# The opening of a Fourier-mixing and hard-swish kernel: zero fills on ScalarE, a third piece buffer, single small transfers, and weight conversions a piece behind, five of them inside chunk 0

## The chip, the cores and the metric

One core of a Trainium2 chip. The metric is the device time of one execution in microseconds (us), lower is better. Traces come from one profiled execution of each kernel, and times in them are us from the first instruction.

## The reference, cut to what matters

```python
x = (8, 3008, 256) float32; w_in = (256, 2048); w_out = (2048, 256)
X = np.fft.fft(np.fft.fft(x, axis=1), axis=2).real      # mixing
h = X.reshape(24064, 256) @ w_in
out = (h * np.clip(h + 3, 0, 6) / 6) @ w_out            # (24064, 256)
```

The Fourier transform along the sequence is done in two stages (47 x 64 = 3008). The transform along the 256 channels is folded into `w_in`; `w_out` is turned into seven blocks `G`. Weights are read as 64-bit floats, so each piece is converted on the chip before use.

## The kernel before

The batch is worked in four pairs, each pair in twelve chunks, each chunk in eight steps. A step of the steady part: TensorE makes `u` and `v` (8 matmuls), VectorE and ScalarE make the gated `a`, GpSimd adds parts of `a` into `c`, and TensorE accumulates 14 matmuls. This repeats from about 119 us to the end. Ahead of it stands the opening, where the change is:

```python
for b in range(2):                                   # zero halves of the tables T
    nc.vector.memset(T[(1 - b) * N2:(2 - b) * N2, b], 0.0)
...
for c in range(NXC):                                 # stage 1, eight pieces
    if c + 2 < NXC:
        load_x(first, c + 2)                         # rows and, by a gather, their partners
    load_w(c + 2)
    exponent_a(c)                                    # ScalarE: PM
    fold...                                          # VectorE
    if c > 0:
        join(c - 1)                                  # VectorE: mantissa x exponent
    mantissa(c)                                      # VectorE, two instructions
    for i in range(XC // 2):
        stage1...(first, c, i)                       # TensorE, then evict_z on ScalarE
    exponent_b(c)                                    # TensorE: scores ex
    exponent_c(c)                                    # ScalarE on ex
    if c in (2, 4, 6):
        use_pair(c // 2 - 1)                         # fold_w_in (TensorE) or mix_w_out (VectorE)
load_g(first, 0); load_g(first, 1); load_t(1)
for j in range(NXC, 14):                             # pieces 8 to 13, between the stages
    load_w(j + 2); exponent_a(j); exponent_b(j)
    if j > NXC:
        exponent_c(j - 1)
    join(j - 1); mantissa(j)
    if j % 2 == 0:
        use_pair(j // 2 - 1)
exponent_c(13); join(13); use_pair(6)
...                                                  # stage 2, then chunk 0 with pieces 14 and 15
```

A piece is converted in five moves: ScalarE writes exponent bits into `PM` (`exponent_a`), TensorE makes the scores `ex` of them (`exponent_b`), ScalarE makes a power of two of each (`exponent_c`), VectorE cuts out the mantissa `top` (`mantissa`, two instructions) and multiplies the two (`join`). A pair of pieces then goes through a "fold" of `w_in` (eight matmuls `wps`) or a "mix" of `w_out`. `mix_w_out` is four VectorE instructions, three subtractions and an addition, with both inputs in SBUF; for short I call them subtractions. `ex` takes one of the three score banks that `u` and `v` use. `evict_z` copies a stage-1 result to a buffer `z` (two of them), stores it, and writes one turned column through `zc` with two small transfers:

```python
def evict_z(pr, c, i, ps):
    if i == 0:
        pr.z[c] = zpool.tile([PZ, XC, D], F32, tag="z", name="z")
    ...
def turn_column(pr, c, z):
    zc = zpool.tile([PZ, XC], F32, tag="zc", name="zc")
    nc.scalar.activation(zc[:, 0:n], z[:, 0:n, P], AF.Identity, scale=...)
    for ci in range(2):
        nc.sync.dma_start(out=to[1 - ci, :, 0:n], in_=zc[ci::2, 0:n])
```

## Time and profile before

| | before |
|---|---|
| median of 3 runs | 2009.34 us (2008.16 to 2011.23) |
| span of the profiled run | 2005.7 us |
| first stage-1 matmul | 13.59 |
| last store of stage 1 issued | 58.10 |
| first matmul of stage 2 | 84.08 |
| first gate operation of VectorE ("S0") | 87.89 |
| eighth accumulation of chunk 0 begins ("A7") | 134.74 |

"Cold" below is TensorE at about half the granted clock (0.5 in the windows), "warm" at the full one. I split A7 into S0, the length of the opening, and A7 - S0 = 46.85, the length of chunk 0. The prediction shows the lines of the profile.

### The profile page before, as it was taken

Reading aid. Unit: us, or ns where it says so; the run is one execution under the profiler, and the core shown is the slowest. Engines: PE = TensorE matmul, PEld = TensorE weight load, DVE = VectorE, ACT = ScalarE, POOL = GpSimd, SP = SyncE. Lnnn points to the kernel's source line nnn. Section 1 sums busy time; section 2 is a strip of 40 time slices with the busy share of each in tenths; the row PEclk is TensorE's granted clock in tenths of the full one; section 3 lists DMA queues with packets and bytes.
Section 4 is the critical chain, followed back from the end, with each engine's and each line's share of the span. In section 5 each row is a group of like instructions: output and inputs, shape, how many; then the busy total and the mean of one; then the engine's idle time right before and its main releaser. Section 6 shows DMA issues by size and latency. Waiting matters only on the chain.

```text
span 2005.7 us, 28349 instructions
## 1 busy us (share of the span) xinstructions
PE 1962.5 (98%) x9144; PEld 1686.7 (84%) x9144; DVE 1444.6 (72%) x2707; ACT 694.7 (35%) x1196; POOL 1419.3 (71%) x1612
## 2 busy tenths in 40 slices
PE   8799999999999999999999999999999999999997
PEld 4388888888888888888888888888888888888886
DVE  6677767776777676777777777777678777777775
ACT  5433333333333333333333333333333333333322
POOL 3277778786677787777658877778666667667665
PEclk8899999999999999999999999999999999999999
DMA  9502211111111122210111221112110101101100
GB/s 294 143 21 56 59 39 47 49 47 35 27 35 50 40 49 53 54 51 25 41 26 29 67 55 42 51 43 52 35 27 19 27 17 26 33 12 27 27 12 19
DMA packets 159560, 93.52 MB, mean 47 GB/s; under 512 B 131595, under 2 KB 144395, under 8 KB 159414
## 3 DMA queue, kind: packets, MB, share of 16 engines
q1 hardware_dynamic: 149942, 58.23, 11.6%
q0 software_dynamic: 9472, 33.49, 6.0%
q8 instruction: 74, 1.21, 0.3%
q14 instruction: 72, 0.59, 0.1%
HBM read 54.32 MB, written 37.33 MB: 46 GB/s over the span
## 4 chain that ended last, share of the span: by engine, by line
PE 92%; DVE 3%; ACT 1%; issue 1%; POOL 0%; SPq 0%; DMA 0%; DVEq 0%; POOLq 0%; ACTq 0%
PE acc L378 55%; PE v L324 16%; PE u L324 16%; PE ps L279 2%; PE ps L226 2%; DVE a L356 1%; ACT t L353 1%; DVE u L337 1%; DVE s L329 1%; PE wps L520 0%; ACT PM L456 0%; DVE o L404 0%; DVE v L343 0%; PE awake L537 0%; PE ps L223 0%
## 5 line engine op out<-in xcount | busy, mean ns | idle before, releaser
L368 POOL TENSOR_TENSOR c<-a 128x512 f32<-128x512 f32 (+1 forms) x384 | 478.9, 1247 | 446.4 <-PE acc L378 361.3
L378 PE MATMUL acc<-c,G 128*128 128x256 f32 (+1 forms) x3072 | 712.1, 375 | 0.0
L353 ACT ACTIVATE t<-u,half 128x512 f32<-128x512 f32 (+2 forms) x416 | 272.3, 654 | 1101.1 <-DVE u L337 1089.5
L378 PEld LDWEIGHTS acc<-c,G 128*128 128x128 f32 x3072 | 577.5, 190 | 72.7
L329 DVE SCALAR_TENSOR_TENSOR s<-qn,WN,u 128x256 f32<-128x256 f32 x768 | 334.5, 477 | 351.6 <-PE u L324 348.8
L378 PE MATMUL acc<-a,G 128*128 128x256 f32 (+1 forms) x2304 | 550.6, 374 | 0.0
L378 PEld LDWEIGHTS acc<-a,G 128*128 128x128 f32 x2304 | 433.8, 190 | 57.4
L324 PE MATMUL v<-q,W 127*128 127x256 f32 x1536 | 397.0, 380 | 8.0 <-DVE a L356 8.0
L324 PE MATMUL u<-q,W 128*128 128x256 f32 x1536 | 394.3, 379 | 0.0
L324 PEld LDWEIGHTS v<-q,W 127*128 127x128 f32 x1536 | 289.5, 190 | 55.7 <-PE u L324 8.4
L324 PEld LDWEIGHTS u<-q,W 128*128 128x128 f32 x1536 | 287.3, 190 | 57.8 <-issue 13.9
L356 DVE SCALAR_TENSOR_TENSOR a<-t,u 128x512 f32<-128x512 f32 (+2 forms) x416 | 266.2, 646 | 95.2 <-ACT t L353 90.5
L368 POOL TENSOR_TENSOR c<-c,a 128x256 f32<-128x256 f32 (+1 forms) x384 | 275.2, 717 | 30.1
L368 POOL TENSOR_TENSOR c<-a,c 128x256 f32<-128x256 f32 (+1 forms) x384 | 275.0, 716 | 30.1
L337 DVE TENSOR_TENSOR u<-s,v 128x512 f32<-128x512 f32 (+1 forms) x384 | 263.0, 685 | 41.1 <-DVE s L329 1.4
L353 ACT ACTIVATE t<-v,half 128x512 f32<-128x512 f32 (+1 forms) x384 | 257.0, 669 | 5.8 <-DVE v L343 4.3
L343 DVE TENSOR_TENSOR v<-v,s 128x512 f32<-128x512 f32 (+1 forms) x384 | 257.7, 671 | 1.1
L356 DVE SCALAR_TENSOR_TENSOR a<-t,v 128x512 f32<-128x512 f32 (+1 forms) x416 | 255.2, 620 | 0.4 <-ACT t L353 0.2
L368 POOL TENSOR_TENSOR r<-w,e 128x256 f32<-128x256 f32 (+1 forms) x96 | 92.2, 981 | 3.8
L384 ACT ACTIVATE e<-acc 128x512 f32<-128x512 f32 (+1 forms) x192 | 86.9, 542 | 2.9 <-PE acc L378 2.8
L404 DVE STREAM_TRANSPOSE o<-r 128x256 f32<-128x256 f32 (+1 forms) x192 | 72.4, 414 | 6.4 <-POOL r L368 6.4
L236 ACT COPY z<-ps 96x512 f32<-96x512 f32 x64 | 36.9, 581 | 82.4 <-PE ps L226 64.1
(81 smaller groups left out, 750.2 us busy)
## 6 DMA issues: line engine op xcount, KB each, us to landing
out_dram<-o SPq DMA_DIRECT2D x736, 32.0 KB
zd<-z SPq DMA_DIRECT2D x32, 384.0 KB
g<-zd SPq DMA_DIRECT2D x48, 256.0 KB
xt<-in_x_dram POOLq DMA_DIRECT2D x21, 384.0 KB, 3.8
qn<-qd SPq DMA_DIRECT2D x23, 256.0 KB
st<-in_moe_w_in_dram POOLq DMA_DIRECT2D x8, 512.0 KB, 9.6
st<-in_moe_w_out_dram POOLq DMA_DIRECT2D x8, 512.0 KB, 5.2
xt<-in_x_dram POOLq DMA_DIRECT2D x7, 376.0 KB, 3.9
```

Source lines behind the costliest of these rows:

```text
L226: nc.tensor.matmul(ps[0:PZ], F[0:PR, 0:PZ], y[:, 2 * i:2 * i + 2, :], start=True, stop=True)
L279: nc.tensor.matmul(ps[:, blk, 2 * u:2 * u + 2], g[:, kk, blk * (P + 1):blk * (P + 1) + P], T[:, :, gr, blk, kk], start=True, stop=True)
L324: nc.tensor.matmul(ps[:, i], W1[r, blk, f * P:(f + 1) * P], q[r, blk, of:of + KC], start=True, stop=True)
L329: nc.vector.scalar_tensor_tensor(s[:, i].rearrange("p k n -> p (k n)"), qn[:, of * N2:(of + KC) * N2], WN[:, f:f + 1], u[:, i].rearrange(" ...
L337: nc.vector.tensor_tensor(u[:, :, 0:ns], s[:, :, 0:ns], v[:, :, 0:ns], op=AL.add)
L343: nc.vector.tensor_tensor(v[:, :, 0:nm], v[:, :, 0:nm], s[:, :, 0:nm], op=AL.subtract)
L353: nc.scalar.activation(t, h, AF.Relu, bias=half[:], scale=scale)
L356: nc.vector.scalar_tensor_tensor(dst, t, 1.0, h, op0=AL.min, op1=AL.mult)
L368: nc.gpsimd.tensor_tensor(out, in0, in1, op=AL.add)
L378: nc.tensor.matmul(ch.acc[i // 2][:, i % 2, 0:ch.n], G[:, i, fc, :], mv, start=(fc == 0 and i % 2 == 0), stop=(fc == NF - 1), skip_group_c ...
L384: nc.scalar.mul(ch.e[:, k:i + 1, 0:ch.n], ch.acc[i // 2][:, 0:i + 1 - k, 0:ch.n], 1.0 / WS)
L404: nc.vector.transpose(o[:, 0:n // DH, h], ch.r[:, m, h, 0:n].rearrange("p (j i) -> p j i", i=DH))
```

## The change

Its intent: start TensorE sooner and warm (fills to ScalarE, piece 0 issued first), not let stores hold ScalarE (third buffer, taken from the idle pool `g`), save issue time (one small transfer), and shorten the stretch between the stages by converting only pieces 7 to 10 there, and 11 to 15 inside chunk 0. The diff also lets `load_g` issue its two rows before its two columns. Core of the diff, with cuts:

```diff
+            pool, tag = (gpool, "g") if pr.p == 0 and c % 3 == 2 else (zpool, "z")
+            pr.z[c] = pool.tile([PZ, XC, D], F32, tag=tag, name="z")
...
-        for ci in range(2):
-            nc.sync.dma_start(out=to[1 - ci, :, 0:n], in_=zc[ci::2, 0:n])
+        nc.sync.dma_start(out=pr.zq[:, :, ::-1, cs].rearrange("b k c n -> (b k) c n"), in_=zc[:, 0:n])
...
-    nc.vector.memset(PM[:], 0x6400)
+    nc.vector.memset(PM[:]....bitcast(I32), 0x64006400)     # and ahead of the table cast
...
-        nc.vector.memset(T[(1 - b) * N2:(2 - b) * N2, b], 0.0)
+        nc.scalar.copy(t, Z[r].unsqueeze(1).to_broadcast([N2, NG, 2 * TB]))
...
+    BEHIND = [0, 1, 2, 3, 4, None, 5, 6]
+    # issue order: piece 0, w 0, piece 1, w 1, piece 2, w 2; load_t(0) after piece 0
+    def next_weights(j):
+        done = pending.pop() if pending else None
+        if done is not None:
+            exponent_c(done)
+        if j is not None:
+            exponent_a(j)
+            mantissa(j)
+        if done is not None:
+            join(done)
+        if j is not None:
+            exponent_b(j)
+            pending.append(j)
+        if done is not None and done % 2:
+            use_pair(done // 2)
...
+    for j in range(7, 11):
+        if j + 3 < 16:
+            load_w(j + 3)
+        next_weights(j)
...
+            for t, j in enumerate([11, 12, 13, 14, 15, None]):   # steps 0 to 5 of chunk 0
+                after.setdefault(t, []).append((next_weights, (j,)))
```

More of the change, by code (lines that the diff above doesn't have):

```diff
@@ L230, in evict_z @@
         if i == 0:
-            pr.z[c] = zpool.tile([PZ, XC, D], F32, tag="z", name="z")
+            pool, tag = (gpool, "g") if pr.p == 0 and c % 3 == 2 else (zpool, "z")
+            pr.z[c] = pool.tile([PZ, XC, D], F32, tag=tag, name="z")
             if c == 0:
@@ L251, in turn_column @@
         nc.scalar.activation(zc[:, 0:n], z[:, 0:n, P], AF.Identity, scale=F[0:PZ, 5 * PZ + NP * NXC:])
-        to = pr.zq[:, :, :, c * XC:(c + 1) * XC].rearrange("b k c n -> c (b k) n")
-        for ci in range(2):
-            nc.sync.dma_start(out=to[1 - ci, :, 0:n], in_=zc[ci::2, 0:n])
+        cs = slice(c * XC, c * XC + n)
+        nc.sync.dma_start(out=pr.zq[:, :, ::-1, cs].rearrange("b k c n -> (b k) c n"), in_=zc[:, 0:n])
         if n < XC:
-            for ci in range(2):
-                nc.sync.dma_start(out=to[ci, :, n], in_=z[ci::2, n, P])
+            nc.sync.dma_start(out=pr.zq[:, :, :, c * XC + n].rearrange("b k c -> (b k c)"), in_=z[:, n, P])
     def load_g(pr, gr):
@@ L262, in load_g @@
         ks = slice(gr * 2 * KK, (gr + 1) * 2 * KK)
+        gb = [g[b * N2:(b + 1) * N2] for b in range(2)]
         for b in range(2):
-            gb = g[b * N2:(b + 1) * N2]
-            nc.sync.dma_start(out=gb[:, :, 0:D], in_=pr.zd[b].rearrange("k c n d -> (c n) k d")[:, ks, :])
-            nc.sync.dma_start(out=gb[:, :, D], in_=pr.zq[b].rearrange("k c n -> (c n) k")[:, ks])
+            nc.sync.dma_start(out=gb[b][:, :, 0:D], in_=pr.zd[b].rearrange("k c n d -> (c n) k d")[:, ks, :])
+        for b in range(2):
+            nc.sync.dma_start(out=gb[b][:, :, D], in_=pr.zq[b].rearrange("k c n -> (c n) k")[:, ks])
         pr.g[gr] = g
@@ L543 @@
     nc.sync.dma_start(out=F[:], in_=c_stage1)
+    bias = wpool.tile([P, 2], F32, tag="bias", name="bias")
+    for i in range(2):
+        nc.vector.memset(bias[:, i:i + 1], (2 * i - 1) * 7.5 / 16.0 - 896.0)
+    nc.vector.memset(half[:], 0.5)
+    PM = wpool.tile([P, 2, 2, WB], I16, tag="PM", name="PM")
+    nc.vector.memset(PM[:].rearrange("p j i n -> p (j i n)").bitcast(I32), 0x64006400)
     nc.vector.tensor_copy(IX[:], F[:, 5 * PZ:5 * PZ + NP * NXC])
@@ L549 @@
     nc.sync.dma_start(out=C[:], in_=dim[:, :, 0:D])
-    load_t(0)
-    load_forward(first, 0)
-    load_forward(first, 1)
-    load_partners(first, 0)
-    load_w(0)
-    load_partners(first, 1)
-    load_w(1)
-    bias = wpool.tile([P, 2], F32, tag="bias", name="bias")
-    for i in range(2):
-        nc.vector.memset(bias[:, i:i + 1], (2 * i - 1) * 7.5 / 16.0 - 896.0)
-    nc.vector.memset(half[:], 0.5)
-    PM = wpool.tile([P, 2, 2, WB], I16, tag="PM", name="PM")
-    nc.vector.memset(PM[:], 0x6400)
     E = wpool.tile([P, 2, P], F16, tag="E", name="E")
@@ L567 @@
     for b in range(2):
-        nc.vector.memset(T[(1 - b) * N2:(2 - b) * N2, b], 0.0)
+        r = slice((1 - b) * N2, (2 - b) * N2)
+        t = T[r, b].rearrange("p g a k n -> p g (a k n)")
+        nc.scalar.copy(t, Z[r].unsqueeze(1).to_broadcast([N2, NG, 2 * TB]))
     wn = dpool.tile([NWI, WB], F32, tag="wn", bufs=1, name="wn")
-    for c in range(NXC):
-        if c + 2 < NXC:
-            load_x(first, c + 2)
-        load_w(c + 2)
-        exponent_a(c)
+    BEHIND = [0, 1, 2, 3, 4, None, 5, 6]
+    load_forward(first, 0)
+    load_partners(first, 0)
+    load_w(0)
+    load_x(first, 1)
+    load_w(1)
+    load_x(first, 2)
+    load_w(2)
+    pending = []
+    def next_weights(j):
[12 more added lines that the diff above has]
+            use_pair(done // 2)
+    for c in range(NXC):
+        if c + 3 < NXC:
+            load_x(first, c + 3)
+            if BEHIND[c + 3] is not None:
+                load_w(BEHIND[c + 3])
+        else:
+            load_w(c + 2)
         on_pe = c not in (2, 4, NXC - 1)
@@ L581 @@
                 fold(first, c, part, nc.vector)
-        if c > 0:
-            join(c - 1)
-        mantissa(c)
+        j = BEHIND[c]
+        done = pending.pop() if pending and j is not None else None
+        if done is not None:
+            exponent_c(done)
+        if j is not None:
+            exponent_a(j)
+            mantissa(j)
+        if done is not None:
+            join(done)
         for i in range(XC // 2):
             (stage1_first if on_pe else stage1)(first, c, i)
-        exponent_b(c)
-        exponent_c(c)
-        if c in (2, 4, 6):
-            use_pair(c // 2 - 1)
+        if j is not None:
+            exponent_b(j)
+            pending.append(j)
+        if done in (1, 3, 5):
+            use_pair(done // 2)
+        if c == 0:
+            load_t(0)
         if c in (3, 5):
@@ L593 @@
     load_g(first, 0)
+    for j in range(7, 11):
+        if j + 3 < 16:
+            load_w(j + 3)
+        next_weights(j)
+    load_wn(PIECES[6][1])
     load_g(first, 1)
     load_t(1)
-    for j in range(NXC, 14):
-        if j + 2 < 16:
-            load_w(j + 2)
-        exponent_a(j)
-        exponent_b(j)
-        if j > NXC:
-            exponent_c(j - 1)
-        join(j - 1)
-        mantissa(j)
-        if j % 2 == 0:
-            use_pair(j // 2 - 1)
-    exponent_c(13)
-    join(13)
-    use_pair(6)
-    load_wn(PIECES[6][1])
     load_wn(PIECES[8][1])
@@ L631, in beside @@
         if p == 0:
-            for t, fs in enumerate([[(f, 14) for f in (exponent_a, exponent_b, mantissa)],
-                                    [(exponent_c, 14), (join, 14)] + [(f, 15) for f in (exponent_a, exponent_b, mantissa)],
-                                    [(exponent_c, 15), (join, 15), (use_pair, 7)]]):
-                after.setdefault(t, []).extend((f, (j,)) for f, j in fs)
+            for t, j in enumerate([11, 12, 13, 14, 15, None]):
+                if j and j + 3 < 16:
+                    after.setdefault(t, []).append((load_w, (j + 3,)))
+                after.setdefault(t, []).append((next_weights, (j,)))
             for gr in range(2, NG):
```

## The prediction

> **What bounds the kernel now.** I read the page's busy shares first, then the table of ten-microsecond windows, then the chain of waits by time, and last the timeline of the opening.
>
> ```profile
> PE 1962.5 (98%) x9144; PEld 1686.7 (84%) x9144; DVE 1444.6 (72%) x2707; ACT 694.7 (35%) x1196; POOL 1419.3 (71%) x1612
> ```
>
> TensorE is busy 98% of the span. After the opening nothing but less matmul work could help, and the change touches no matmul of the main loop. The windows show where TensorE is not the bound (columns: window, length, busy PE, PEld, DVE, ACT, POOL, then clock, DMA share, GB/s):
>
> ```profile
> 10.00:20.00 10.00, 6.41 (x15) 4.27 (x16) 6.03 (x9) 2.00 (x3) 4.20 (x6) 0.68 1.02 282
> 40.00:50.00 10.00, 10.00 (x41) 6.45 (x40) 5.98 (x15) 6.96 (x14) 1.06 (x2) 1.00 1.02 352
> 70.00:80.00 10.00, 6.31 (x13) 2.24 (x12) 4.11 (x11) 6.98 (x12) 1.50 (x2) 0.84 0.80 200
> 100.00:110.00 10.00, 9.09 (x42) 7.45 (x41) 9.54 (x15) 3.62 (x6) 7.25 (x8) 1.00 0.00 1
> ```
>
> Up to 50 us the transfers are full (share 1.02); from 60 to 80 nothing is full, so a chain of waits runs; from 90 to 118 VectorE is (0.95). The chain of waits by time says where each ends:
>
> ```profile
> 53.77 1.13 PE ps L226 x2
> ...
> 65.99 0.48 ACT ex L465
> 66.47 1.35 ACT PM L456 x2
> ...
> 68.24 5.14 PE wps L520 x8
> ...
> 79.53 4.71 PE awake L537 x8
> 84.24 1.78 PE ps L279 x16
> ...
> 119.75 3.02 PE acc L378 x14
> ```
>
> The last piece of stage 1 runs at 53.8, weight conversions hop between ScalarE and TensorE until 79.5, stage 2 starts at 84, and from 118.6 on every link is TensorE, one step (14 matmuls "acc", 8 of u and v) each 4.75 us (119.75 to 124.50). So the change is worth exactly what it takes off or puts onto the time at which this steady row starts.
>
> **What the Trainium skill says.** (1) TensorE: Matmul & The Clock Gate, Part 1: the array runs at half rate until some 3.4 us of activity and falls back after an idle window of that size. The trace agrees on size, not on time: the last warming matmuls are issued 0.43 us apart, TensorE then idles 4.0 us, and from 13.59 the stage-1 matmuls come 0.85 apart until about 24.1, over ten microseconds. (2) SBUF — State Buffer, "Who interferes with whom": a VectorE instruction with two SBUF inputs, or one in a two-port mode, excludes a reading GpSimd instruction and the other way round. The trace agrees: a mantissa pair costs 0.42 + 0.69 alone and 0.65 + 1.64 beside GpSimd's sums. (3) ScalarE: Activation LUTs, "What ACT_TABLE_LOAD costs": 186 ns + 0.833 ns per element. For 512 elements that is 0.61; the trace has 0.58. (4) DMA: Bandwidth & Descriptors, Specifications: about 358 GB/s of HBM for a core; the fullest window here has 352.
>
> **The change part by part.**
>
> *Zero fills.* VectorE spends 6.41 to 12.3 on two fills of 64x3072 (2.62 each), and the first fold starts at 12.24, directly behind:
>
> ```profile
> 9.70 2.62 DVE L568 MEMSET T<- 64x3072 f32 x1 [0.68 <-issue]
> 12.24 0.62 DVE L188 TENSOR_TENSOR y<-xt 94x508 f32<-94x508 f32 x1
> ```
>
> On ScalarE each costs 0.19 + 3072 x 0.833 ns = 2.75 us (estimate after the skill), 5.5 together, from 4.1 to 9.6, where ScalarE had waited 9.7 us for weights: free. But GpSimd's next issue, which waited for a gather, went at 12.32, so the partner rows of piece 0 landed only about then. The new issue order puts piece 0 first: ahead of that gather are 0.39 MB (piece 1) and 0.26 MB (first table T) less, at 0.28 MB/us 2.3 us. First fold about 9.3 instead of 12.24, first stage-1 matmul about 10.7 instead of 13.59. TensorE then idles about 1 us and stays at full clock, which returns up to half of the 10.5 cold us, 5 us.
>
> *Can stage 1 use it?* TensorE had hardly a gap from 13.6 to 50.7, 37.1 us, of which about 5.2 were cold loss: 32 us of work, so from 10.7 it could be through piece 6 near 43. The stream is the next limit. The last gather was issued at 34.04 and such loads land a median 12.1 us later: 46. About 13.3 MB had moved by then. In the new order one weight piece fewer (0.52 MB) precedes it, and the outputs of stage 1 leave earlier and fill the slower first 25 us; I put it at 43.6. Then the fold (51.16 to 53.8: 2.6 us), its matmuls (53.77 to 57.45: 3.7, part of it cold), the copy (0.6): the last store of stage 1 goes at about 50.3 instead of 58.10, a gain of 8 us.
>
> *Third buffer, one small transfer.* ScalarE waited for old stores 1.6 us in total, and a pair of small issues takes 1.12 against about 0.56 for one. Both lie beside other work, and the big last store, landing about 3.7 after issue, holds back the reload anyway. Together 0 to 1 us; I count 0.5.
>
> *Conversions between the stages.* Before, pieces 8 to 13 followed: 58.1 to 79.3. Now 7 to 10 do. On ScalarE: exponent 0.58 + PM 1.40 + wait 0.6 + exponent 0.58 + PM 1.40 = 4.6, then TensorE's fold of w_in: 0.5 + 3.6 warm or 5.3 cold (68.08 to 73.4 was cold), a copy 0.6; then the same again without the copy. From 50.3: 54.9, 61.3, 65.9, 71.7. The warming matmuls, 3.5 if warm, end at 75.2 and stage 2 starts there instead of 84.08. Gain so far 8.9; with both folds warm 12.
>
> *Conversions in chunk 0.* Here it is paid. Before, from the first gate operation at 87.89 VectorE's rounds start at 91.58, 95.27, 101.21, 107.73, 115.26, 119.01: a bare round is 3.7, one with a mantissa 5.9, with mantissa and join 6.5, with join and mix (four subtractions, 3.0 beside GpSimd, 1.65 alone) 7.5.
>
> ```profile
> 98.95 0.65 DVE L473 TENSOR_SCALAR top<-st 128x512 int32<-128x512 int32 x1
> 99.64 1.64 DVE L474 SCALAR_TENSOR_TENSOR top<-st,top 128x512 f32<-128x512 uint32 x1
> 101.21 0.86 DVE L329 SCALAR_TENSOR_TENSOR s<-qn,WN,u 128x256 f32<-128x256 f32 x2
> ```
>
> After, steps 0 to 4 each have mantissa and join, steps 1 and 3 a mix too, step 5 join and mix. GpSimd's sums (2.7 us, begun 0.3 after the gates) cover mantissa and join, so a mix behind them runs at about 1.7 to 2: 3 x 6.5 + 2 x 8.2 + 7.2 = 43.1 us. The same six rounds before are 5.94 + 6.52 + 7.53 + 3.75 = 23.7 and two at TensorE's pace, 9.7: 33.4. Extra 9.7. Piece 10 also keeps one of three score banks over the first two rounds, about 0.4 each: 0.8. Given back: 10.5.
>
> *Sum.* -8.9 - 0.5 + 10.5 = +1. TensorE is as busy as before afterwards, so nothing more happens in the other 1880 us.
>
> **The rivals.** *A: chunk 0 hides the conversions.* VectorE has 1.05 us of slack per step at TensorE's pace and GpSimd's collisions may be fewer. For it: mantissa and mix cost half when alone. Against: VectorE is at 0.95 in that window already, and a step with a conversion also has a path of 6.5 us over ScalarE (scores, exponent, PM) and TensorE. If it holds, 5 us come back there: 2004. *B: the opening gains less, because the stream sets stage 1's end.* For it: share above 1.0 until 50 us. Against: the last fold started 5 us after its rows could have landed. Then 4 us less: 2014. *C: the reload of stage-2 input becomes the last wait before stage 2*, as its 4-byte pieces are slow. Issued at about 54 to 57, it would have to take over 15 us; before it waited for nobody visibly. Worth +3 at most. *D: warm clock throughout*: the wait chain gains 3 us more: 2006.
>
> **Range and chances.** The two large terms, -9 (sd about 3) and +10.5 (sd about 3), are nearly equal and opposite. D and A both point down, only B and C up, and my rounds for chunk 0 take every collision; I lean 2.5 us below the sum: 2007.5 against 2009.34. Range 1999 to 2016, some 4 us of one sigma widened for noise (the three runs span 3 us). Two per cent is 40 us, a third of the whole opening of 118 us, of which a large part is matmul work and transfers that stay: faster 0.01, slower 0.01, within 0.98.
>
> **What would show it.** Right: first fold near 9 to 10 us and stage-1 matmuls 0.43 apart from the start; the last stage-1 store near 50; stage 2 near 75; VectorE over 0.95 busy for six rounds, steps of 6.5 and 8 us; steady 4.75 us row starting within a few us of 118.6 plus the same two steps. Wrong: matmuls still cold at 13 to 24; last gather landing after 46; TensorE waiting for the reload; or rounds in chunk 0 near 5 us, which would mean that the collision and not the instruction count had been the price.

## The result, and the profile after

The changed kernel took 2020.77 us (median of 4 runs, 2019.13 to 2022.19) against 2009.81 (4 runs) for the kernel before: ratio 1.0055, 95% interval 1.0037 to 1.0072. A ratio is the mean time of one kernel's runs over that of the other's runs of the same rounds, so it is not quite the ratio of the medians quoted. It is slower by half a per cent, within the 2% called "same", and outside my range of 1999 to 2016.

| | before | after | predicted |
|---|---|---|---|
| first fold | 12.24 | 9.76 | 9.3 |
| first stage-1 matmul | 13.59 | 11.19 | 10.7 |
| last store of stage 1 | 58.10 | 53.79 | 50.3 |
| stage 2 starts | 84.08 | 77.32 | 75.2 |
| S0 | 87.89 | 81.14 | about 79 |
| A7 - S0 | 46.85 | 66.30 | 10.5 more than before |
| A7 | 134.74 | 147.44 | +1 |

A7 moved by 12.7 and the span by 13.2 (2005.7 to 2018.9): nearly the whole loss lies before A7. The opening gained 6.75; chunk 0 lost 19.45.

The busy shares and the windows of the changed kernel, in the columns of those shown before:

```profile
PE 1966.6 (97%) x9144; PEld 1686.5 (84%) x9144; DVE 1447.8 (72%) x2705; ACT 700.3 (35%) x1198; POOL 1422.2 (70%) x1612
```
```profile
10.00:20.00 10.00, 7.79 (x35) 5.44 (x36) 5.43 (x12) 5.17 (x9) 4.31 (x6) 1.00 1.03 259
40.00:50.00 10.00, 8.47 (x37) 5.65 (x36) 5.66 (x17) 4.82 (x9) 0.53 (x1) 1.00 1.05 343
70.00:80.00 10.00, 10.00 (x41) 5.85 (x39) 0.00 (x0) 2.34 (x4) 0.00 (x0) 0.91 0.34 68
100.00:110.00 10.00, 8.37 (x35) 5.91 (x34) 9.58 (x15) 3.10 (x5) 5.91 (x5) 1.00 0.16 52
110.00:120.00 10.00, 7.38 (x32) 5.87 (x31) 7.51 (x13) 4.84 (x8) 3.10 (x3) 0.83 0.00 0
```

The first row shows the good part: from 10 to 20 the granted clock is 1.00 instead of 0.68 and 35 matmuls run instead of 15. The last two show the bad one: from 100 to 110 VectorE is nearly full (9.58) and TensorE has gaps; from 110 to 120 neither is full (7.51 and 7.38), so a chain of waits runs there, and TensorE's clock falls to 0.83. The chain of waits by time of the changed kernel, chunk 0:

```profile
102.71 1.65 DVE top L475
...
107.55 1.31 DVE G L512
...
112.31 1.33 ACT PM L457 x2
113.63 0.04 issue
113.68 0.59 PE ex L462
114.26 1.71 PE ps L280 x8
115.97 1.07 PE u L325 x4
...
124.83 1.37 DVE G L511
126.20 1.40 DVE G L512
...
142.55 2.43 PE acc L379 x10
```

The steady row of TensorE begins at 142.55 and no longer at 118.6. Between stand mantissas (`top L475`), mixes (`G L51x`), and once the path from ScalarE's PM over the scores, a piece of stage 2 and `u`.

VectorE's rounds (start of one `s` to the next) carry the comparison. The first two come ahead of step 0, so round 3 belongs to step 0, round 4 to step 1, and so on:

| round | 1 | 2 | 3 | 4 | 5 | 6 | 7 | 8 |
|---|---|---|---|---|---|---|---|---|
| before | 3.69 | 3.69 | 5.94 | 6.52 | 7.53 | 3.75 | 4.66 | 4.75 |
| predicted | 4.1 | 4.1 | 6.5 | 8.2 | 6.5 | 8.2 | 6.5 | 7.2 |
| after | 4.40 | 5.93 | 6.78 | 10.53 | 8.29 | 10.45 | 6.44 | 8.80 |

Sums: 40.5 before, 51.3 predicted, 61.6 after. The plain conversion rounds 3 and 7 are right; the three rounds with a mix (4, 6, 8) are 6.2 too long, rounds 1 and 2 are 2.1, and round 5 is 1.8. Here is VectorE in round 4 of the changed kernel, and GpSimd at the same time:

```profile
102.26 0.42 DVE L474 TENSOR_SCALAR top<-st 128x512 int32<-128x512 int32 x1
102.71 1.65 DVE L475 SCALAR_TENSOR_TENSOR top<-st,top 128x512 f32<-128x512 uint32 x1
104.28 0.74 DVE L490 TENSOR_TENSOR G<-top,ex 128x256 f32<-128x256 f32 x2
104.94 0.41 DVE L509 TENSOR_TENSOR G<-G,b 128x256 f32<-128x256 f32 x1
105.39 0.83 DVE L510 TENSOR_TENSOR G<-G 128x256 f32<-128x256 f32 x1
106.26 1.37 DVE L511 TENSOR_TENSOR G<-G 128x256 f32<-128x256 f32 x1
107.55 1.31 DVE L512 TENSOR_TENSOR G<-G,b 128x256 f32<-128x256 f32 x1
```
```profile
102.50 1.31 POOL L369 TENSOR_TENSOR c<-a 128x512 f32<-128x512 f32 x1 [2.77 <-DVE a L357]
103.89 1.06 POOL L369 TENSOR_TENSOR c<-c,a 128x256 f32<-128x256 f32 x1
105.02 0.92 POOL L369 TENSOR_TENSOR c<-a,c 128x256 f32<-128x256 f32 x1
105.90 1.44 POOL L165 TENSOR_TENSOR xt<-xt 94x508 f32<-94x508 f32 x1
107.31 1.26 POOL L166 TENSOR_TENSOR xt<-xt 94x508 f32<-94x508 f32 x1
```

A subtraction of the same size takes 0.41 at 104.94 and 1.37 at 106.26. Each of the three long ones ends 0.28 or 0.29 us after a GpSimd instruction ends: 106.22 after 105.94, 107.63 after 107.34, 108.86 after 108.57 (start plus length in the lines above). The join at 104.28, which reads one input from PSUM, keeps its length. So I had GpSimd's sums in my rounds, but not the fold of the next pair's piece that follows them in steps 3 and 5.

### The profile page after: what moved, and what is told of

It reads as the page before. It is cut to its first block, busy times and chain, and to the rows that moved or that the text cites. A ratio compares the mean times of both kernels' runs of the same rounds, so it can differ in the third digit from the quotient of the medians.

```text
span 2018.9 us, 28294 instructions
## 1 busy us (share of the span) xinstructions
PE 1966.6 (97%) x9144; PEld 1686.5 (84%) x9144; DVE 1447.8 (72%) x2705; ACT 700.3 (35%) x1198; POOL 1422.2 (70%) x1612
## 3 DMA queue, kind: packets, MB, share of 16 engines
q1 hardware_dynamic: 149366, 58.22, 11.7%
## 4 chain that ended last, share of the span: by engine, by line
PE 92%; DVE 3%; DMA 2%; ACT 1%; issue 1%; POOL 0%; SPq 0%; DVEq 0%; POOLq 0%; ACTq 0%
PE acc L379 54%; PE v L325 16%; PE u L325 16%; PE ps L280 2%; PE ps L226 2%; DVE a L357 1%; PE wps L521 1%; DMA zq<-zc 1%; DMA xt<-in_x_dram,IX 1%; DVE u L338 1%; ACT t L354 1%; ACT PM L457 0%; DVE s L330 0%; DVE top L475 0%; DVE o L405 0%
## 6 DMA issues: line engine op xcount, KB each, us to landing
st<-in_moe_w_in_dram POOLq DMA_DIRECT2D x8, 512.0 KB, 10.7
```

## The experiments

Twelve kernels in three calls, four to a call. Within a call they share the runs of the kernel before; ratios are always to it. My theory after the result: the five conversions inside chunk 0 are the loss, and about half of their cost is VectorE standing behind GpSimd. Rivals: another part of the opening costs; chunk 0 is slow for TensorE's clock, or only for the number of instructions.

How far a single trace can be trusted: stage 1 is the same program in the changed kernel and in seven of these runs (two_inside, none_inside, five_flushed, folds_later, exp_order, sums_written, two_order), and its last store went anywhere from 51.91 to 54.73. So a shift of that store or of S0 by less than 3 us between two traces shows nothing. Lengths are steadier: chunk 0 agrees within 0.2 us in the kernels that have the same conversions there (46.85 to 47.03, and 66.30 to 66.41).

### Call 1: which part of the change loses

**two_inside**: 11 to 13 converted between the stages as well, the last one joined there.

```diff
-    for j in range(7, 11):
+    for j in range(7, 14):
...
+    next_weights(None)
-            for t, j in enumerate([11, 12, 13, 14, 15, None]):
+            for t, j in enumerate([14, 15, None]):
```

> The changed kernel with only pieces 14 and 15 converted inside chunk 0, as before the change; 11 to 13 stand between the stages and the last one there is joined before stage 2. Theory (the five conversions inside chunk 0 are the loss): stage 2 starts about 6 us later than in the changed kernel (77.5 to 83.5), but the stretch from the first gate operation to the eighth step falls from 66 to about 47 us, so the run is 12 to 14 us faster than the changed kernel, ratio to before 0.999 to 1.001. Rival (another part of the opening costs: the single small transfer, the third buffer, the clock): it stays 5 us or more slower than before, ratio 1.003 or more.

Measured: 2012.61 us, ratio 1.0017 (1.0000 to 1.0033). Chunk 0 is back at 47.01, and about 8 of the 11 us are regained, not the 12 to 14 expected: the conversions inside chunk 0 are most of the loss, and the two intervals do not overlap. But stage 2 starts at 88.23 instead of the expected 83.5, and S0 is 92.05, later than before (87.89), although the last store went earlier (54.02). So the rival holds too, for 3 us: the stretch between the stages has become longer. One cause is in the edit: seven pieces (7 to 13) stand there, in the kernel before six (8 to 13).

**none_inside**: the same edit with `range(7, 16)` and an empty list.

> All sixteen pieces are converted before stage 2. Theory: stage 2 starts 9 to 11 us later than in the changed kernel, chunk 0 runs at TensorE's 4.75 us a step after the first two rounds (41 us from the first gate operation to the eighth step), so ratio to before 0.997 to 1.000, and at least as fast as two_inside. Rival (conversions inside chunk 0 are mostly hidden, the loss is elsewhere): slower than two_inside by some 4 us, ratio 1.004 or more.

Measured: 2012.59 us, ratio 1.0018 (1.0002 to 1.0035). S0 is 96.81, chunk 0 is 42.94. A piece moved out of chunk 0 cost (96.81 - 92.05) / 2 = 2.4 and gave (47.01 - 42.94) / 2 = 2.0: a draw for the last two pieces. For the three before, chunk 0 paid (66.30 - 47.01) / 3 = 6.4 each. The expected ratio of at most 1.000 was missed for the same reason as in two_inside.

**five_flushed**: five inside, but piece 10 is joined before stage 2.

```diff
         next_weights(j)
+    next_weights(None)
```

> Five inside as in the changed kernel, but piece 10 is joined before stage 2, so that its score bank is free when the first two rounds of chunk 0 want it. Theory (the pinned bank makes rounds 1 and 2 4.4 and 5.9 us instead of 3.7): 2.5 to 4 us faster than the changed kernel, ratio to before 1.0035 to 1.0045. Rival (the first rounds are slow because TensorE's clock is cold or for lack of data): no difference, 1.0055.

Measured: 2017.22 us, ratio 1.0042 (1.0025 to 1.0059). Rounds 1 and 2 fall to 3.69 and 3.69, chunk 0 from 66.30 to 62.82. The bank that piece 10 kept cost 3.5 us of chunk 0 as the trace shows it; the intervals of the two kernels' ratios overlap.

**folds_later**: GpSimd's folds of the next pair in steps 6 and 7 of chunk 0.

```diff
-                put(9 * c + 3, fold, nx, c, 0, nc.gpsimd)
-                put(9 * c + 5, fold, nx, c, 1, nc.gpsimd)
+                late = 3 if p == 0 and c == 0 else 0
+                put(9 * c + 3 + late, fold, nx, c, 0, nc.gpsimd)
+                put(9 * c + 5 + late - late // 3, fold, nx, c, 1, nc.gpsimd)
```

> Five inside as in the changed kernel, but GpSimd's two folds for the next pair move from steps 3 and 5 of chunk 0 to steps 6 and 7, away from the mixes. Theory (mix rounds cost 10.5 us since four two-input subtractions collide with GpSimd's sums and, in steps 1 and 3, with a fold): the two mix rounds fall to about 9 each, 3 us faster, ratio 1.004. Rival (the mix rounds wait for something else, TensorE or ScalarE): under 1 us, 1.0055.

Measured: 2017.03 us, ratio 1.0035 (1.0018 to 1.0052). Rounds 4 and 6 fall from 10.53 and 10.45 to 8.70 and 9.17, chunk 0 to 62.67. VectorE's mix in round 4 of this kernel:

```profile
106.42 0.41 DVE L509 TENSOR_TENSOR G<-G,b 128x256 f32<-128x256 f32 x1
106.87 0.84 DVE L510 TENSOR_TENSOR G<-G 128x256 f32<-128x256 f32 x1
107.74 0.42 DVE L511 TENSOR_TENSOR G<-G 128x256 f32<-128x256 f32 x1
108.08 0.42 DVE L512 TENSOR_TENSOR G<-G,b 128x256 f32<-128x256 f32 x1
```

From 106.42 to 108.50 it is 2.1 us long, close to the 1.7 to 2 that my prediction had assumed, where the changed kernel needs 3.9. The ratio's interval overlaps that of the changed kernel, so it is the trace that carries this reading. Only the third subtraction's and the fourth's neighbours on GpSimd are gone.

### Call 2: what became slower between the stages, and what the start is worth

In the chain of two_inside two waits stand out. First, ScalarE's order. Its conversions between the stages, then those of the kernel before:

```profile
78.44 1.40 ACT L457 ACTIVATE PM<-st,bias 128x512 uint8<-128x512 int16 x2
80.31 0.58 ACT L466 ACTIVATE ex<-ex 128x512 int32<-128x512 f32 x1 [0.46 <-PE ex L462]
80.80 1.41 ACT L457 ACTIVATE PM<-st,bias 128x512 uint8<-128x512 int16 x2
```
```profile
75.70 1.39 ACT L456 ACTIVATE PM<-st,bias 128x512 uint8<-128x512 int16 x2
76.99 0.58 ACT L465 ACTIVATE ex<-ex 128x512 int32<-128x512 f32 x1
77.51 1.39 ACT L456 ACTIVATE PM<-st,bias 128x512 uint8<-128x512 int16 x2
```

"A piece behind" does `ex` of piece j - 1, then PM of piece j. But the PM of j - 1 was ScalarE's last instruction, and TensorE needs it for the scores that `ex` reads; so ScalarE waits, and a piece takes 2.36 (78.44 to 80.80) instead of 1.81 (75.70 to 77.51). Second, in the changed kernel ScalarE waits for the small transfer of two pieces before:

```profile
50.70 0.30 ACT L253 ACTIVATE zc<-z,F 96x4 f32<-96x4 f32 x1 [2.12 <-DMA zq<-zc]
50.90 0.57 ACT L466 ACTIVATE ex<-ex 128x512 int32<-128x512 f32 x1
```

**zc_three**: the changed kernel with `bufs=3` for the tile `zc`.

> The changed kernel with a third buffer for the small column tile as well. In its trace ScalarE waited 2.1 us (3.4 in two_inside) for the small transfer of two pieces before, which had been under way for 12.7 us, and the last pieces of stage 1 wait behind it. Theory (that wait sits on the path to the last store of stage 1): the store goes 2 to 3 us earlier (53.8 to about 51.3) and the run is 2 to 3 us faster than the changed kernel, ratio to before 1.004 to 1.0045. Rival (the stream of pieces ends stage 1 anyway): no change, 1.0055.

Measured: 2018.94 us, ratio 1.0042 (1.0028 to 1.0056). The wait is gone from ScalarE's list. The last store goes at 52.63 instead of 53.79 and S0 is 79.93, but that is within the spread of the same stage 1 given above, and 1.8 us of medians taken in different calls is within what the intervals leave open. A gain from this buffer is not shown.

**exp_order**: the changed kernel, with the old order between the stages only.

```diff
+        if j is not None and starting[0]:
+            exponent_a(j)
         if done is not None:
             exponent_c(done)
-        if j is not None:
+        if j is not None and not starting[0]:
             exponent_a(j)
+        if j is not None:
             mantissa(j)
```

> The changed kernel, but between the stages ScalarE does the PM of the next piece before the exponent of the last, as the kernel before did; in the changed order it does nothing while TensorE makes the scores. Theory (each such turn costs the wait of 0.5 to 0.65 us that the trace shows twice among four pieces): stage 2 starts 1 to 1.5 us earlier, ratio 1.0045 to 1.005. Rival (TensorE's fold of w_in hides the order): no change, 1.0055.

Measured: 2017.62 us, ratio 1.0038 (1.0025 to 1.0052). From the last store to S0 it takes 24.9 us (53.06 to 77.97) instead of 27.35 (53.79 to 81.14): 2.4 us, more than the 1 to 1.5 expected from the exposed waits alone, and outside the 27.3 to 28.0 of the four traces with the changed order (the changed kernel, zc_three, folds_later, sums_written).

**two_zc_order**: two_inside with both mends.

> two_inside with both mends: third column buffer and the old order between the stages. Theory (two_inside stays 3.4 us behind the kernel before for these two reasons): stage 2 starts 5 us earlier than in two_inside (88.2 to about 83), ratio to before 0.998 to 1.000. Rival (what keeps it behind is that one more piece stands after stage 1 and that TensorE is cold there): at most 2 us better, 1.001 or more.

Measured: 2005.25 us, ratio 0.9977 (0.9963 to 0.9991). It is faster than the kernel before, by 0.2%, and than the changed one. S0 is 85.24 (92.05 in two_inside), chunk 0 is 47.02. Stage 2 starts 6.8 us earlier than in two_inside (81.43), where 5 were expected.

**start_only**: the kernel before with the fills on ScalarE, piece 0 issued first, and the first table after piece 0; `PM` and the small constants are also filled earlier, as in the change.

> The kernel before with only the beginning of the change: zero fills on ScalarE, piece 0 issued first, first table after piece 0. Theory (the start is a gain of its own: TensorE begins at 11.2 with a full clock instead of 13.6 with half): the last store of stage 1 goes 3 to 5 us earlier (58.1 to 53 to 55) and the run is 3 to 5 us faster than before, ratio 0.9975 to 0.9985. Rival (the stream of pieces sets the end of stage 1): within 1 us of before, 1.000.

Measured: 2005.79 us, ratio 0.9982 (0.9968 to 0.9996). So the start is a gain of its own, 3.6 us by the ratio (0.8 to 6.4 by its interval). The way was not as expected: the last store went at 57.23, only 0.9 earlier, and ScalarE waited 5.9 us for old stores (`z <- zd`); S0 came 1.4 earlier (86.45) in the profiled run, which at 2004.0 was 1.7 under the profiled run of before. Where the rest of the ratio comes from one trace does not show.

### Call 3: collisions or count, and the small parts

**sums_written**: in chunk 0 of the first pair GpSimd writes zeros instead of adding, so it reads nothing for its sums. Its output is wrong, which doesn't matter for the time.

```diff
+        if ch.pr.p == 0 and ch.ck == 0:
+            for k in (slice(0, 2), 2, 3):
+                nc.gpsimd.memset(cn[:, k], 0.0)
+        else:
             add(cn[:, 0:2], ...)      # and the other two sums
```

> Wrong on purpose: the changed kernel with five conversions inside, but in chunk 0 of the first pair GpSimd writes zeros where it would read and add, so that it issues as many instructions and reads nothing for them. Theory (VectorE's mantissas and mixes in chunk 0 are slow because GpSimd reads at the same time): a mantissa falls from 2.0 to about 1.1 us, a mix from 3.9 to under 3 (the folds of the next pair still read), the stretch from the first gate operation to the eighth step falls from 66 to 56 to 60, and the run is 6 to 10 us faster than the changed kernel, ratio 1.001 to 1.0025. Rival (the number of instructions and TensorE's wait for scores set the rounds): under 3 us, 1.004 or more.

Measured: 2010.37 us, ratio 1.0007 (0.9994 to 1.0021), relative error 0.17. VectorE in round 4 of this kernel (its lines are numbered four higher):

```profile
101.78 0.42 DVE L478 TENSOR_SCALAR top<-st 128x512 int32<-128x512 int32 x1
102.24 0.69 DVE L479 SCALAR_TENSOR_TENSOR top<-st,top 128x512 f32<-128x512 uint32 x1
102.84 0.74 DVE L494 TENSOR_TENSOR G<-top,ex 128x256 f32<-128x256 f32 x2
103.50 0.42 DVE L513 TENSOR_TENSOR G<-G,b 128x256 f32<-128x256 f32 x1
...
104.76 0.42 DVE L516 TENSOR_TENSOR G<-G,b 128x256 f32<-128x256 f32 x1
```

The second mantissa instruction takes 0.69 instead of 1.65, the mix 1.7 (103.50 to 105.18) instead of 3.9. Chunk 0 takes 54.62 instead of 66.30, and the changed kernel is 10 us faster with the same number of VectorE instructions: 90 from S0 to A7 in both, busy for 56.0 us there and for 45.4 here. So GpSimd's sums cost the changed kernel's chunk 0 about 12 us, and the mere number of instructions does not explain the loss.

Three limits go with this. First, the edit also shortened GpSimd's work (33.5 to 13.2 us busy in that stretch) and moved it: the folds `xt` now run from 99.46 to 101.77, ahead of the mix, and GpSimd is idle during the mix. That reading is what blocks, and not GpSimd being at work, shows at the mantissas only: the one at 102.24 runs beside GpSimd's zero writes (102.00 to 103.17) and still takes 0.69. Second, the kernel before has such collisions too, some 3.8 us by its lines (two mantissa pairs of 2.3 instead of 1.15, a mix of 3.2 instead of 1.7). So of the 19.5 us some 8 are collisions that the change added (my estimate, 11.7 less 3.8); the same edit to the kernel before was not run. Third, TensorE's clock: from S0 to A7 it was 1.00 in the kernel before, 0.90 in the changed kernel, 0.97 here. In the changed kernel it fell after waits of TensorE (2.32 us before 89.39, 2.56 before 113.03); the four matmuls of `u` at 89.39 took 2.04 instead of 1.10. So the rival of the clock is not refuted: it adds to what the waits cost, and no run separates it.

The rounds are now 4.40, 4.85, 6.94, 7.01, 7.16, 7.01, 6.19 and 5.94. In this run's chain rounds 3, 5 and 7 go over `PM`, scores and `u`, as round 5 of the chain above does; rounds 4 and 6, with a mix, still go through VectorE.

**two_order**: two_inside with the old order alone.

> two_inside with the old order between the stages alone, without the third column buffer. The two mends together took 7 us off two_inside. Theory (four exposed waits of 0.65 us for scores, and the column wait of 2 to 3 us): 3 us faster than two_inside, ratio 1.000 to 1.001. Rival (the order carries nearly all of it): 0.998.

Measured: 2007.21 us, ratio 0.9992 (0.9979 to 1.0006), 5 us under two_inside by the medians, more than the 3 expected. From the last store to S0 it takes 31.97 against 38.03, more than seven exposed waits of 0.55 explain. Part of it is TensorE's clock: by the two chains the second group of `wps` matmuls took 5.14 in two_inside and 3.69 here, the warming matmuls 5.55 and 4.46. The kernel before needs 29.79; the 2.2 left are about what a seventh piece there costs (2.4 in none_inside). The third column buffer then accounts for at most the rest (0.9992 to 0.9977), and the intervals overlap.

**mended_two_small**: two_zc_order with the two small transfers of before.

> two_zc_order with two small transfers for each piece again, as before the change. Theory (the single transfer saves only issue time of an engine that waits anyway): within 1 us of two_zc_order, ratio 0.997 to 0.9985. Rival (single transfers help the path): 2 us slower, 0.999 or more; or, if the single one lands later, faster, under 0.997.

Measured: 2005.77 us, ratio 0.9978 (0.9964 to 0.9992), S0 85.29 against 85.24. The single transfer is worth nothing that these runs can show; the intervals are some 3 us wide to each side.

**mended_two_z**: two_zc_order with `pool, tag = zpool, "z"`, two piece buffers as before.

> two_zc_order without the third buffer for first-stage pieces. Theory (with TensorE started early the pieces come faster than their stores land, start_only showed 5.9 us of ScalarE waiting for them): 2 to 4 us slower than two_zc_order, ratio 0.999 to 1.000. Rival (the stream of pieces sets the pace, the buffer is idle): within 1 us, 0.997 to 0.9985.

Measured: 2008.10 us, ratio 0.9991 (0.9977 to 1.0004). ScalarE waits 11.1 us for old stores (in two_zc_order not at all), the last store goes at 56.30 instead of 53.67, S0 is 88.37 instead of 85.24. The store is later than in any of the eight traces of the same stage 1 with three buffers (51.91 to 54.73), so the trace speaks for 2 to 4 us of worth; the ratios' intervals overlap, so the size is not settled.

## Why the prediction was right or wrong

- **The bound, and what the change can move**: right. Only the time at which the steady row begins moved, and the span followed it.
- **Small slips of the sums**: two rounds at TensorE's pace are 9.4 (4.66 and 4.75), not 9.7; with the sum of +1 the lean gives 2007.8 and rivals A and D 2005.3 and 2007.3, not 2007.5, 2004 and 2006. None of them decides anything.
- **Zero fills and start**: right. ScalarE did the two fills in 5.51 us (5.5 estimated), the first fold came at 9.76 (9.3), the matmuls are 0.43 apart at once. That they stay so (rival D) was wrong: the clock was 0.51 from 24 to 27 and 0.50 from 52 to 60.
- **End of stage 1**: the step "from 10.7 it could be through piece 6 near 43" failed. It added up TensorE's work without gaps. TensorE waited 2.38 us for the gather and fold of piece 2, ran the next matmuls cold again, and was through piece 6 at 47.4; then ScalarE's column wait of 2.1 us followed. Nor did the last gather go earlier, as the landing put at 43.6 required: it was issued at 34.01, before at 34.04. Last store 53.8 instead of 50.3.
- **Third buffer, one small transfer** ("I count 0.5"): the transfer shows no worth, the buffer more than I gave it, some 2 to 4 us by its trace (in mended_two_z ScalarE waits 11.1 us for old stores, in the kernel before 1.6).
- **Conversions between the stages**: the length of 24.9 us from last store to stage 2 (50.3 to 75.2) was nearly right, 23.5 measured. I had written the wait of 0.6 for scores into the chain without asking whether the kernel before has it. It has not; this, and one piece more that stands there, is why moving pieces back out (two_inside) did not bring the opening of before.
- **Conversions in chunk 0**: this is the step that broke the range. "So a mix behind them runs at about 1.7 to 2" and "given back: 10.5" became 19.45. The mechanism was right in one half: VectorE collides with GpSimd. The other half, VectorE over 0.95 busy for six rounds, was not: from S0 to A7 it was busy 56.0 of 66.3 us (0.84) and waited about 7 us for TensorE's `u` and `v`. The terms of the sum were mis-sized. Rounds with a mix were 10.5, 10.5 and 8.8 instead of 8.2, 8.2 and 7.2: in the first two GpSimd's folds come right behind its sums (folds_later brings the mix down to 2.1), and in the third VectorE waited 1.38 us for `v`, which was cold (2.07 for four matmuls, 1.03 when warm). The kept bank cost 3.5, not 0.8 (five_flushed). Round 5, the conversion in step 2, took 8.3, since a half of stage 2 stands between scores and `u` on TensorE, which the "path of 6.5 us" left out, and it ran partly cold: 1.71 us by the chain, 0.89 at 144.98.
- **The lean of 2.5 us below the sum**: wrong, and argued from rivals D and A without new evidence. A ("chunk 0 hides the conversions") is refuted by two_inside and none_inside, 6.4 us of chunk 0 for each piece moved in; B's number (the opening gains less) came true, its reason, the stream of pieces, is not shown; C (the reload becomes the last wait) did not: the chain goes from the warming matmuls straight to stage 2.

Round 2 of the changed kernel, 5.93 after 4.40 in the first, is answered: with the bank free (five_flushed) both are 3.69, and in round 2 TensorE, after waiting for the bank, ran `u` cold. Still open: what the cold clock alone cost in chunk 0, and where start_only's gain beyond the 1.4 us of its trace lies.

## What to carry to other kernels

Before work is moved into a stretch that looks hidden, list what every engine does in that very stretch, the far ones too: a VectorE instruction that is 0.4 us long alone was 1.4 us long beside a GpSimd fold that belonged to the next pair and was in nobody's sum. A change made of many parts is worth undoing part by part: here a good start (0.9982 alone) was buried under one bad placement, and the version with the placement undone and two small mends ran at 0.9977. The intervals of these two nearly coincide, so beyond the start no part of the change is shown to gain. And "one piece behind" is only behind if the engine has other work between a value's request and its use; on ScalarE the order of two instructions made a conversion 2.36 instead of 1.81 us.

## What the Trainium skill lacked or had wrong

- TensorE: Matmul & The Clock Gate, Part 1: after an idle window a busy window of some 3.4 us brings the full clock back. In the kernel before TensorE was busy from 13.59 on and its matmuls stayed at 0.85 us until about 24.1, more than 10 us. With an idle gap of 1.5 us (changed kernel, before 11.19) the clock stayed full, as the page has it; but a gap of 2.38 us (20.43 to 22.81), shorter than the page's idle window, was followed by half the clock (0.51 from 24 to 27).
- SBUF — State Buffer, "Who interferes with whom": the rule held (a VectorE instruction with two SBUF inputs waits for a GpSimd instruction that reads; with GpSimd only writing it does not: 1.65 against 0.69). The page has no size for a chain of such waits: four subtractions of 0.42 took 3.9 us beside back-to-back GpSimd reads, 2.1 beside a part of them and 1.7 with GpSimd idle.
- No page that I read says how long a small transfer takes behind a full stream: a column of 96 x 4 floats, issued at 37.90 with the DMA share above 1.0, landed 12.7 us later by the chain of waits.
